# Pins, grouped routing and interleaved first expert products in a fused attention and two-layer expert kernel

## The chip, the cores and the metric

The kernel runs on one core of one Trainium2 chip. The metric is device time in microseconds (us) of one execution. Lower is better. The core has TensorE (PE, matrix products), VectorE (DVE), ScalarE (ACT), GpSimd (POOL) and SyncE (SP, which issues most of the transfers). Each engine runs its own instructions in one fixed order and waits for the others by semaphores.

## The reference, cut to what matters

Three layers follow one another on 3072 tokens of 512 values.

```python
# 1. attention, 4 x 8 heads of 64: 8 global keys and a causal window of 96, with a linear bias
a = softmax(where(keep, q @ k.T / 8 + bias, -1e9)); x = (a @ v)              # [3072, 512]
# 2. a dense pair of layers
h = x @ w_in;  g = where(h > 0, h, exp(min(h, 0)) - 1);  y = g @ w_out       # 512 -> 2048 -> 512
# 3. eight experts, the best one for each token that is to be computed at all
chosen = y @ w_skip > 0;  logits = y[chosen] @ w_gate;  e = argmax(logits)
gate = softmax(logits)[e]
out = y;  out[chosen] += gate * (relu(y @ w1[e]) @ w2[e])                    # 512 -> 1024 -> 512
```

## The kernel before, in words

**Groups and steps.** The 3072 tokens are 24 tiles of 128, in eight groups `m` of three tiles. For each group, `program` (L807) walks over sixteen slices `f` of the 2048 hidden values. One step `(m, f)` issues `moe_h(m, f)` (L429: twelve products of 384 columns, then ScalarE, VectorE, ScalarE and GpSimd in a chain that makes the half-precision pair `gs`) and, two steps behind it (`LAG`, L50), `moe_y` (L451: nine products of 512 columns). Between the steps of groups 0 to 6 stand pieces of the attention of the next group (`att_step`, L357). Numbers are split into two half-precision parts, so that each product is made of three.

**The check of the first weights.** The weights of the layer pair arrive as pairs of 32-bit words and are rebuilt in `w_prep` (L399) during group 0. Later they are loaded a second time and checked: 16 loads of 1 MB (`w_load(f, "wc")`, L393) and 32 VectorE operations (`w_check`, L419, the operation on L425), of which the program text has one every second step of groups 2 to 5 (L889 to L893). A load is written down four steps ahead of its first check, the very first one two steps ahead. The loads use the two buffers `stage`, which the expert weights use later (L595).

**Routing.** `route(m)` (L488) returns pieces that later steps call one by one: `evac` copies the three results out of PSUM, `turn` splits a tile and turns it by a transposing transfer, `gate` makes nine logits for one tile (eight products into `lg`, then eleven VectorE operations and one ScalarE exponential, per tile), `place` counts ranks with two products into `rk` and finds each token's slot with twelve VectorE operations per tile, `scatter` writes a tile's rows into the DRAM tensor `xg` by an indirect transfer from GpSimd. Scatters into one tensor wait for each other. `write` copies the last group's rows to the output.

**The experts.** `ex_tail` (L681) has steps too. Steps 0 to 47 take the first 128 slots of experts 0, 1 and 2 (steps 0 to 23) and then their second 128 slots (steps 24 to 47), eight slices each; after them come experts 3 to 7. A step issues `ex_first` (L638, twelve products), one weight split per tile (`prep`, L848, which calls `ex_prep`, L603) and, two steps behind, `ex_second` (L658, three products per tile). The rows of a tile come from `xg` by `ex_gather` (L620) and are split and turned by `ex_tokens` (L628): two VectorE operations (L634, L635) into the single buffer `yh`, then a transposing transfer into `eyT`. The routing pieces of the last group stand between these steps, by `ROUTE_LAST` (L60). When an expert's tile is done, L674 makes the result, L676 turns the token number into an index `ix` (two buffers, L675), and L677 scatters the rows to the output.

**What sets the order.** The program text isn't the order on the engines. A scheduler at build time simulates the kernel and puts on each engine what is ready first by its own times; an operation whose inputs it takes as early can be put far ahead of its place in the text. `pin` (L72) prevents that: a pinned instruction comes behind the one that was written just before it on its engine. It adds order, not a wait. Before the change the ScalarE half of each weight split is pinned (L613), but not the loads and operations of the check, nor L634.

Of the kernel before, what the change touches and what calls it, by code (L numbers as in the profile page):

```python
# [19 lines left out]
P = 128  # L20
# [39 lines left out]
ROUTE_LAST = {0: 'et', 4: 'A', 5: 'B', 6: 'C', 8: 'p', 9: 'sw'}  # L60


class Fast:
# [424 lines left out]
    def route(self, m):  # L488

        nc, mp = self.nc, self.mp  # L490
        sm = mp.tile([P, TB, 32], F32, tag="sm", name=f"sm_{m}", bufs=2)
        oh = mp.tile([P, TB, E], F16, tag="oh", name=f"oh_{m}", bufs=2)
        yts, yTs, poss = {}, {}, {}
# [24 lines left out]

        def gate(t):
            n = m * TB + t  # L520
            yt = yts[t]
            lg = self.ps.tile([P, 2, E + 1], F32, tag=f"s{t % 2}", name=f"lg_{n}", bufs=1)
# [4 lines left out]
            q = sm[:, t, :]  # L527
            L = mp.tile([P, E + 1], F32, tag="L", name=f"L_{n}", bufs=2)
            nc.vector.tensor_scalar(L, lg[:, 1, :], 1.0 / (RS * GS), None, ALU.mult)
            nc.vector.scalar_tensor_tensor(L, lg[:, 0, :], 1.0 / (RS * GS), L, ALU.mult, ALU.add)  # L530
            m8 = mp.tile([P, 8], F32, tag="m8", name=f"m8_{n}", bufs=2)
            mi = mp.tile([P, 8], U32, tag="mi", name=f"mi_{n}", bufs=2)
            nc.vector.max(m8, L[:, 0:E])
            nc.vector.max_index(mi, m8, L[:, 0:E])

            nc.vector.tensor_scalar(q[:, 0:1], m8[:, 0:1], -1.0, None, ALU.mult)
            nc.scalar.activation(q[:, 8:16], L[:, 0:E], AF.Exp, bias=q[:, 0:1], accum_out=q[:, 1:2])

            nc.vector.scalar_tensor_tensor(q[:, 7:8], L[:, E:E + 1], 0.0, q[:, 1:2], ALU.mult, ALU.add)
            nc.vector.tensor_tensor(self.esum[:, t:t + 1], self.esum[:, t:t + 1], q[:, 7:8], ALU.add)  # L540
            nc.vector.tensor_copy(q[:, 2:3], mi[:, 0:1])
            nc.vector.tensor_scalar(q[:, 3:4], L[:, E:E + 1], 0.0, None, ALU.is_gt)
            nc.vector.tensor_scalar(oh[:, t, :], self.iota8, q[:, 2:3], q[:, 3:4], ALU.is_equal, ALU.mult)

        def place():
            rk = self.ps.tile([P, 2, TB, E], F32, tag="s1", name=f"rk_{m}", bufs=1)
            for x in range(2):
                nc.tensor.matmul(rk[:, x], self.tri[:, x, :], oh, start=True, stop=True)
            for t in range(TB):
                n = m * TB + t  # L550
                q, yt = sm[:, t, :], yts[t]
                nc.vector.tensor_tensor(q[:, 16:24], rk[:, 0, t, :], self.carry, ALU.add)
                nc.vector.tensor_tensor_reduce(q[:, 24:32], q[:, 16:24], oh[:, t, :], 1.0, 0.0,
                                               ALU.mult, ALU.add, q[:, 4:5])
                nc.vector.tensor_tensor(self.carry, self.carry, rk[:, 1, t, :], ALU.add)
# [125 lines left out]
    def ex_tail(self, prep):  # L681
# [8 lines left out]
        for s_, (e, f, tiles) in enumerate(steps):  # L690
# [23 lines left out]
            for _ in tiles:  # L714
                prep()
# [457 lines left out]
```

## Time and profile before

| | |
|---|---|
| median of 3 runs | 878.21 us (876.48 to 879.97) |
| the profiled execution | 877.69 us; its span on the chip 876.0 us |
| PE busy | 818.5 us, 93% |
| DVE, ACT, POOL busy | 604.8, 535.9, 176.3 us |
| mean granted TensorE clock | 0.978 of full speed |
| moved by transfers | 148.80 MB, mean 170 GB/s |
| the sixteen DMA engines' share for SP's transfers | 62.6% |

A share is a mean over stages that differ: attention and weight loading at first, the steady steps of the layer pair in the middle, the experts at the end. The stretches below are given in us from the start of the span. Group 1 ends its results with the evacuation at 248.5 us, and the last group with that at 678 us.

### The profile page before, as it was taken

To read this page: it belongs to the slowest core of one execution; us is meant where nothing else is said; L and a number is where in the kernel's file an instruction comes from. 1 tells how busy PE (TensorE), PEld (TensorE's weight loads), DVE (VectorE), ACT (ScalarE), POOL (GpSimd) and SP (SyncE) were. 2 spreads that over 40 slices of the span, in tenths; PEclk is the share of its full clock that TensorE was granted. 3 is DMA by queue.
4 is the path that set the end of the run, shared out by engine and by line. 5 is a ranking of instruction groups with operands and counts; after the bars stand their busy time and mean duration, and the time that the engine had idled before them with its cause. 6 is when DMAs were issued, how large, how long until landed. Compare 5 with 4: busy or idle time off the path is not lost.

```text
span 876.0 us, 17838 instructions
## 1 busy us (share of the span) xinstructions
PE 818.5 (93%) x6177; PEld 476.3 (54%) x6177; DVE 604.8 (69%) x2263; ACT 535.9 (61%) x1326; POOL 176.3 (20%) x201
## 2 busy tenths in 40 slices
PE   6998888889999999999999999999998879999995
PEld 5774444445555555555555555555553646766663
DVE  6997897778767647756755765652786957876632
ACT  4775766566777767777767777654665635554311
POOL 1001112112312322312231231132232011100100
PEclk9998899899999999999999999999999999999998
DMA  8999999999875445457546543630546787878410
GB/s 290 270 281 263 223 268 254 249 268 312 212 142 112 109 121 120 113 103 155 114 96 115 109 78 69 111 65 13 168 147 185 225 247 240 263 241 239 134 43 25
DMA packets 185396, 148.80 MB, mean 170 GB/s; under 512 B 152209, under 2 KB 154257, under 8 KB 181201
## 3 DMA queue, kind: packets, MB, share of 16 engines
q1 hardware_dynamic: 182096, 141.59, 62.6%
q0 software_dynamic: 3200, 5.99, 1.9%
q8 instruction: 50, 0.82, 0.4%
q14 instruction: 50, 0.40, 0.2%
HBM read 94.82 MB, written 21.08 MB: 132 GB/s over the span
## 4 chain that ended last, share of the span: by engine, by line
PE 61%; DMA 13%; DVE 12%; issue 11%; POOL 1%; ACT 1%; SPq 0%; POOLq 0%; DVEq 0%; ACTq 0%
PE h L437 23%; PE y L458 21%; PE s L239 5%; DMA out<-eres,ix 5%; PE pv L324 4%; PE eh L650 3%; PE eo L666 3%; DMA xg<-yt,pos 2%; PE warm L354 2%; DMA yTs<-yh 1%; DVE wt L406 1%; DVE wt L407 1%; DMA wc<-in_wf 1%; DVE e L444 1%; DVE w L414 1%
## 5 line engine op out<-in xcount | busy, mean ns | idle before, releaser
L437 PE MATMUL h<-xT,w 128*128 128x384 f16 x1536 | 277.2, 331 | 5.3 <-DMA xT<-xs 3.6
L458 PE MATMUL y<-w,gs 128*128 128x512 f16 x1152 | 271.5, 380 | 3.7 <-POOL gs L448 1.9
L448 POOL TENSOR_TENSOR gs<-e,gs 128x384 f16<-128x384 f32 x128 | 126.8, 992 | 420.0 <-ACT gs L447 364.9
L437 PEld LDWEIGHTS <-w 128*128 128x128 f16 x1536 | 147.4, 99 | 109.4 <-issue 13.7
L458 PEld LDWEIGHTS <-gs 128*128 128x128 f16 x1152 | 110.5, 98 | 125.1 <-POOL gs L448 3.4
L447 ACT ACTIVATE gs<-e 128x384 f16<-128x384 f32 x128 | 66.9, 523 | 97.2 <-DVE e L444 96.3
L444 DVE SCALAR_TENSOR_TENSOR e<-e,h 128x384 f32<-128x384 f32 x128 | 70.5, 551 | 73.7 <-ACT e L442 71.0
L253 ACT ACTIVATE p<-p,st 128x232 f32<-128x232 f32 (+1 forms) x192 | 89.3, 466 | 39.8 <-DVE st L248 39.5
L666 PE MATMUL eo<-ew,ehs 128*128 128x512 f16 x384 | 101.7, 385 | 6.7 <-DVE ehs L654 6.6
L650 PE MATMUL eh<-eyT,ew 128*128 128x128 f16 (+1 forms) x1152 | 101.8, 239 | 4.9 <-DMA eyT<-eyh 3.4
L650 PEld LDWEIGHTS <-ew 128*128 128x128 f16 x1152 | 86.8, 99 | 31.3 <-issue 5.5
L614 DVE SCALAR_TENSOR_TENSOR ew<-er,ew 128x512 f16<-128x512 f32 x128 | 88.8, 711 | 9.3 <-ACT ew L613 8.6
L441 ACT ACTIVATE e<-h 128x384 f32<-128x384 f32 x128 | 61.5, 480 | 45.7 <-PE h L437 38.5
L652 ACT ACTIVATE ehs<-eh 128x128 f16<-128x128 f32 (+1 forms) x96 | 30.0, 312 | 96.1 <-PE eh L650 93.5
L248 DVE CUSTOM_DVE_ANT_0 p<-s,tab 128x232 f32<-128x232 f32 (+1 forms) x192 | 67.1, 376 | 18.4 <-PE s L239 15.8
L613 ACT ACTIVATE ew<-er 128x512 f16<-128x512 f32 x128 | 75.5, 620 | 6.7 <-DMA er<-in_moe_w 6.6
L283 DVE TENSOR_TENSOR ph<-p,ph 128x464 f16<-128x464 f32 x68 | 44.2, 663 | 39.5 <-ACT ph L282 39.5
L442 ACT ACTIVATE e<-e 128x384 f32<-128x384 f32 x128 | 66.7, 521 | 3.2
L666 PEld LDWEIGHTS <-ehs 128*128 128x128 f16 x384 | 35.1, 99 | 33.4 <-DVE ehs L654 10.7
L239 PE MATMUL s<-qh 64*128 64x232 f16 (+1 forms) x432 | 40.9, 257 | 10.9 <-DVE st L248 8.4
L654 DVE SCALAR_TENSOR_TENSOR ehs<-eh,ehs 128x128 f16<-128x128 f32 (+1 forms) x96 | 31.7, 331 | 26.0 <-ACT ehs L652 26.0
L677 POOL DMA_INDIRECT out<-eres,ix x16 | 17.1, 1069 | 144.9 <-DVE eres L674 112.5
(172 smaller groups left out, 915.1 us busy)
## 6 DMA issues: line engine op xcount, KB each, us to landing
er<-in_moe_w SPq DMA_DIRECT2D x64, 512.0 KB
wr<-in_wf SPq DMA_DIRECT2D x16, 1024.0 KB
wc<-in_wf SPq DMA_DIRECT2D x16, 1024.0 KB
qk<-in_qk SPq DMA_DIRECT2D x20, 720.0 KB
out<-yt SPq DMA_DIRECT2D x24, 256.0 KB
rawv<-in_vp SPq DMA_DIRECT2D x21, 256.0 KB
xg<-zrow SPq DMA_DIRECT2D x16, 257.0 KB
yg<-xg SPq DMA_DIRECT2D x16, 257.0 KB
```

Source lines behind the costliest of these rows:

```text
L239: nc.tensor.matmul(sp[j], q[r, hp, KW:], k[r, hp, KW - w:KW], start=(x == 0), stop=(x == len(mm) - 1))
L248: nc.vector.tensor_tensor_reduce(pw[:, j, :], sp[j], self.tab[:, h, :] if i else self.tab0[:, h, :], -0.125, 3e38, ALU.add, ALU.min, st[:, ...
L253: nc.scalar.activation(pw[:, j, :], pw[:, j, :], AF.Exp, bias=st[:, 0, h:h + 1], scale=-1.0, accum_out=st[:, 1, h:h + 1])
L437: nc.tensor.matmul(hps, wi[:, s_, c, :], xT[:, x * ND + c, :], start=(n == 0), stop=(n == 3 * ND - 1))
L444: nc.vector.scalar_tensor_tensor(g, e, -HS, hps, ALU.mult, ALU.max, accum_out=self.gsum[:, m * NF + f:m * NF + f + 1])
L447: nc.scalar.activation(gs[:, 0], g, AF.Copy)
L448: nc.gpsimd.tensor_tensor(gs[:, 1], g, gs[:, 0], ALU.subtract)
L458: nc.tensor.matmul(self.ys[m][t], gs[:, s_, t * P:(t + 1) * P], wo[:, x, :], start=(f == 0 and n == 0), stop=(f == NF - 1 and n == 2))
L613: self.pin(nc.scalar.activation(w[:, 0], r, AF.Copy, scale=sc))
L614: nc.vector.scalar_tensor_tensor(w[:, 1], r, sc, w[:, 0], ALU.mult, ALU.subtract, accum_out=self.esums[:, c:c + 1])
L650: nc.tensor.matmul(hps, l, r, start=(i == 0), stop=(i == len(mm) - 1))
L666: nc.tensor.matmul(self.eo[(e, t)], hs[:, s_, j * P:(j + 1) * P], self.ew[(e, 4 + f // 2, f % 2)][:, x, :], start=(f == 0 and n == 0), sto ...
```

## The change

Six edits. (1) The check's loads and operations, and L634, are pinned. (2) The routing's VectorE work is done for three tiles in one operation where it can be; the logits leave PSUM by a ScalarE copy, and the exponential is one operation for three tiles, off the way to the slots. (3) The ranks come from nine products of eight columns instead of two of 24, so that the sum over earlier tiles of the group is made in PSUM. (4) The last two `moe_y` steps of the layer pair move behind the expert steps' first products: steps 0 and 1, `moe_y(7, 14)`, step 2, `moe_y(7, 15)`. For that steps 0 to 2 take their PSUM from `s0`, `s1` and `h` in turn. (5) The routing pieces of the last group, and what follows from them, come three steps later, the second tiles' tokens two steps later. (6) `ix` has 16 buffers.

```diff
-ROUTE_LAST = {0: 'et', 4: 'A', 5: 'B', 6: 'C', 8: 'p', 9: 'sw'}
+ROUTE_LAST = {3: 'et', 7: 'A', 8: 'B', 9: 'C', 11: 'p', 12: 'sw'}
...
-        self.nc.sync.dma_start(t, self.a["wf"].bitcast(I32)[f].rearrange("p k (d t) -> p k d t", t=2))
+        d = self.nc.sync.dma_start(t, self.a["wf"].bitcast(I32)[f].rearrange("p k (d t) -> p k d t", t=2))
+        if name == "wc":
+            self.pin(d)
...
-        self.nc.vector.scalar_tensor_tensor(self.andw, self.wc[:, k, :, 1], 0x40000000, self.andw,
-                                            ALU.bitwise_xor, ALU.bitwise_and)
+        self.pin(self.nc.vector.scalar_tensor_tensor(self.andw, self.wc[:, k, :, 1], 0x40000000, self.andw,
+                                                     ALU.bitwise_xor, ALU.bitwise_and))
...
+            nc.scalar.activation(Lr[:, t], lg, AF.Copy, scale=1.0 / (RS * GS))
+            if t == TB - 1:
+                choose()
+
+        def choose():
+            L = mp.tile([P, TB, E + 1], F32, tag="L", name=f"L_{m}", bufs=2)
+            nc.vector.tensor_tensor(L, Lr[:, :, 0, :], Lr[:, :, 1, :], ALU.add)
...
+            for t in range(TB):
+                nc.vector.max(m8[:, t], L[:, t, 0:E])
+                nc.vector.max_index(mi[:, t], m8[:, t], L[:, t, 0:E])
+            nc.vector.tensor_copy(expert, mi[:, :, 0])
+            nc.vector.tensor_scalar(chosen, L[:, :, E], 0.0, None, ALU.is_gt)
+            nc.vector.tensor_tensor(oh, self.iota8.unsqueeze(1).to_broadcast([P, TB, E]), wide(expert), ALU.is_equal)
+            nc.vector.tensor_tensor(oh, oh, wide(chosen), ALU.mult)
...
+            nc.scalar.activation(z, z, AF.Exp)
+            nc.vector.tensor_reduce(out=esum, in_=z, op=ALU.add, axis=AX.X)
...
+            rk = self.ps.tile([P, TB + 1, E], F32, tag="s1", name=f"rk_{m}", bufs=1)
+            for t in range(TB + 1):
+                for x in range(min(t + 1, TB)):
+                    nc.tensor.matmul(rk[:, t], self.tri[:, 0 if x == t else 1, :], oh[:, x],
+                                     start=(x == 0), stop=(x == min(t, TB - 1)))
...
+            nc.vector.tensor_tensor(z, rk[:, 0:TB], self.carry.unsqueeze(1).to_broadcast([P, TB, E]), ALU.add)
+            nc.vector.tensor_tensor(self.carry, self.carry, rk[:, TB], ALU.add)
+            nc.vector.tensor_tensor(z, z, oh, ALU.mult)
+            nc.vector.tensor_reduce(out=rank, in_=z, op=ALU.add, axis=AX.X)
+
+            nc.vector.scalar_tensor_tensor(check, rank, float(CAP), chosen, ALU.is_lt, ALU.mult)
+            nc.vector.tensor_scalar(check, check, -OOB, OOB, ALU.mult, ALU.add)
+            nc.vector.scalar_tensor_tensor(slot, expert, float(CAP), rank, ALU.mult, ALU.add)
+            nc.vector.tensor_tensor(pos, slot, check, ALU.add)
...
-        nc.vector.tensor_scalar(yh[:, 0], y, RS, None, ALU.mult)
+        self.pin(nc.vector.tensor_scalar(yh[:, 0], y, RS, None, ALU.mult))
...
-            ix = self.xp.tile([P, 1], I32, tag="ix", name=f"ix_{e}_{t}", bufs=2)
+            ix = self.xp.tile([P, 1], I32, tag="ix", name=f"ix_{e}_{t}", bufs=2 * E)
...
-            if s_ == 10:
+            if s_ == 0:
+                self.htags = "s0", "s1", "h"
+            if s_ == 3:
+                self.htags = ("h",)
+            if s_ == 13:
                 self.htags = "h", "s0", "h", "s1"
-            if s_ == 12:
+            if s_ == 15:
                 for x in range(NX):
                     self.ex_gather(x, 1)
             for x in range(NX):
-                if s_ == 20 + 2 * x:
+                if s_ == 22 + 2 * x:
                     self.ex_tokens(x, 1)
...
             self.ex_first(e, f, tiles)
+            if s_ and rest:
+
+                self.moe_y(*rest.pop(0))
...
-        for k in range(LAG):
-            self.moe_y(*steps[k - LAG])
-        self.ex_tail(prep)
+        self.ex_tail(prep, steps[-LAG:])
```

## Rows read from the trace of the kernel before

**Rows 1.** Windows: each engine's busy us (x instructions), granted clock, DMA share, GB/s.

```profile
136.00:167.00 31.00, 25.93 (x163) 12.96 (x161) 21.14 (x59) 17.95 (x46) 6.38 (x6) 0.89 0.86 250
167.00:249.00 82.00, 77.74 (x578) 41.53 (x577) 63.16 (x227) 55.25 (x137) 19.73 (x19) 0.98 0.96 245
249.00:322.00 73.00, 72.92 (x559) 39.45 (x557) 47.76 (x194) 52.51 (x135) 19.23 (x19) 1.00 0.51 120
615.00:679.00 64.00, 60.33 (x341) 30.85 (x340) 46.80 (x186) 39.54 (x84) 17.20 (x18) 1.00 0.55 171
```

**Rows 2.** Windows of the check's operation alone, L425 on DVE.

```profile
136.00:167.00 31.00, 9.55 (x12) 0.89 0.86 250
167.00:249.00 82.00, 15.03 (x20) 0.98 0.96 245
```

**Rows 3.** Timeline of ACT: evacuations; start, us, line, op, tiles, count [idle before].

```profile
167.54 1.07 ACT L499 ACTIVATE yt<-y 128x512 f32<-128x512 f32 x2
248.54 1.07 ACT L499 ACTIVATE yt<-y 128x512 f32<-128x512 f32 x2
322.49 1.07 ACT L499 ACTIVATE yt<-y 128x512 f32<-128x512 f32 x2
```

**Rows 4.** Timeline of DVE: a check behind a load that is late.

```profile
153.96 0.69 DVE L425 SCALAR_TENSOR_TENSOR andw<-wc,andw 128x512 int32<-128x512 int32 x1 [6.01 <-DMA wc<-in_wf]
```

**Rows 5.** Windows behind the idle time of PE that ends at 156 us.

```profile
156.00:160.00 4.00, 3.90 (x14) 1.67 (x14) 3.38 (x12) 3.11 (x10) 0.67 (x1) 0.50 0.75 252
160.00:165.00 5.00, 5.00 (x30) 2.29 (x29) 2.47 (x10) 2.84 (x6) 0.56 (x1) 0.79 1.00 277
```

**Rows 6.** Timeline of DVE: token splits at the end of the layer pair.

```profile
660.58 0.43 DVE L634 TENSOR_SCALAR eyh<-yg 128x512 f16<-128x512 f32 x1 [3.73 <-DMA yg<-xg]
664.96 1.12 DVE L634 TENSOR_SCALAR eyh<-yg 128x512 f16<-128x512 f32 x1 [0.71 <-DMA eyT<-eyh]
```

**Rows 7.** Chain of waits: start, us, what; products, and a gather's landing.

```profile
577.20 0.04 PE rk L548 x2
696.20 0.67 PE eh L650 x12
696.87 0.65 PE eo L666 x3
708.89 2.70 DMA yg<-xg
```

**Rows 8.** Timeline of POOL: the last group's three scatters.

```profile
694.86 0.99 POOL L572 DMA_INDIRECT xg<-yt,pos  x1 [17.25 <-DVE sm L557]
700.34 0.97 POOL L572 DMA_INDIRECT xg<-yt,pos  x1 [4.48 <-ACT ew L613]
705.76 1.37 POOL L572 DMA_INDIRECT xg<-yt,pos  x1 [3.18 <-DMA out<-eres,ix]
```

**Rows 9.** Timeline of DVE: index and token splits in the experts' first steps.

```profile
705.47 0.15 DVE L676 CAST ix<-yg 128x1 int32<-128x1 f32 x1 [5.03 <-DMA out<-eres,ix]
718.86 0.43 DVE L634 TENSOR_SCALAR eyh<-yg 128x512 f16<-128x512 f32 x1 [2.81 <-issue]
```

**Rows 10.** Timeline of DVE: an index that waits, later experts.

```profile
792.21 0.15 DVE L676 CAST ix<-yg 128x1 int32<-128x1 f32 x1 [3.58 <-DMA out<-eres,ix]
```

**Rows 11.** Timeline of PE: products that began after idle time.

```profile
677.67 1.68 PE L458 MATMUL y<-w,gs 128*128 128x512 f16 x7 [0.39 <-POOL gs L448]
720.77 0.39 PE L666 MATMUL eo<-ew,ehs 128*128 128x512 f16 x1 [2.18 <-DVE ehs L654]
798.29 1.48 PE L650 MATMUL eh<-eyT,ew 128*128 128x256 f16 x12 [1.72 <-DMA eyT<-eyh]
820.96 1.47 PE L650 MATMUL eh<-eyT,ew 128*128 128x256 f16 x12 [1.65 <-DMA eyT<-eyh]
```

**Rows 12.** Groups by line: shapes xcount | busy us, mean ns | idle before, releasers.

```profile
L530 DVE SCALAR_TENSOR_TENSOR L<-lg,L 128x9 f32<-128x9 f32 x24 | 4.0, 167 | 0.6
L537 ACT ACTIVATE sm<-L,sm 128x8 f32<-128x8 f32 x24 | 7.2, 298 | 8.9 <-DVE sm L536 8.6
```

More of the change, by code (lines that the diff above doesn't have):

```diff
@@ L490, in route @@
         nc, mp = self.nc, self.mp
-        sm = mp.tile([P, TB, 32], F32, tag="sm", name=f"sm_{m}", bufs=2)
+        sm = mp.tile([P, 7, TB], F32, tag="sm", name=f"sm_{m}", bufs=2)
         oh = mp.tile([P, TB, E], F16, tag="oh", name=f"oh_{m}", bufs=2)
-        yts, yTs, poss = {}, {}, {}
+        pos = mp.tile([P, TB], I32, tag="pos", name=f"pos_{m}", bufs=2)
+        Lr = mp.tile([P, TB, 2, E + 1], F32, tag="Lr", name=f"Lr_{m}", bufs=2)
+        esum, expert, chosen, rank, slot, check, gate_ = (sm[:, x, :] for x in range(7))
+        yts, yTs = {}, {}
         def evac():
@@ L517, in turn, with wide @@
             nc.sync.dma_start_transpose(yTs[t], yh.rearrange("p s d -> p (s d)"))
+        def wide(x):
+            return x.unsqueeze(2).to_broadcast([P, TB, E])
         def gate(t):
-            n = m * TB + t
-            yt = yts[t]
-            lg = self.ps.tile([P, 2, E + 1], F32, tag=f"s{t % 2}", name=f"lg_{n}", bufs=1)
+            lg = self.ps.tile([P, 2, E + 1], F32, tag=f"s{t % 2}", name=f"lg_{m}_{t}", bufs=1)
             for c in range(ND):
@@ L526, in gate @@
                 nc.tensor.matmul(lg[:, 0, :], yTs[t][:, ND + c, :], self.wgs[:, c, 0, :], start=False, stop=(c == ND - 1))
[L527 to L541, printed above, removed]
@@ L542, in gate @@
-            nc.vector.tensor_scalar(q[:, 3:4], L[:, E:E + 1], 0.0, None, ALU.is_gt)
-            nc.vector.tensor_scalar(oh[:, t, :], self.iota8, q[:, 2:3], q[:, 3:4], ALU.is_equal, ALU.mult)
-        def place():
[L546 to L555, printed above, removed]
-                nc.vector.tensor_scalar(q[:, 5:6], q[:, 4:5], float(CAP), None, ALU.is_lt)
-                nc.vector.tensor_tensor(q[:, 5:6], q[:, 5:6], q[:, 3:4], ALU.mult)
-                nc.vector.tensor_scalar(q[:, 5:6], q[:, 5:6], -OOB, OOB, ALU.mult, ALU.add)
-                nc.vector.scalar_tensor_tensor(q[:, 6:7], q[:, 2:3], float(CAP), q[:, 4:5], ALU.mult, ALU.add)
-                nc.vector.tensor_tensor(q[:, 6:7], q[:, 6:7], q[:, 5:6], ALU.add)
-                pos = mp.tile([P, 1], I32, tag="pos", name=f"pos_{n}", bufs=4)
-                nc.vector.tensor_copy(pos, q[:, 6:7])
-                nc.vector.tensor_scalar(q[:, 1:2], q[:, 1:2], 1e-9, RS * E1S * E2S, ALU.add, ALU.mult)
-                nc.vector.reciprocal(yt[:, DM:DM + 1], q[:, 1:2])
-                poss[t] = pos
@@ new lines, in gate @@
+            nc.scalar.activation(Lr[:, t], lg, AF.Copy, scale=1.0 / (RS * GS))
[4 more added lines that the diff above has]
+            nc.vector.tensor_tensor(L, Lr[:, :, 0, :], Lr[:, :, 1, :], ALU.add)
+            m8 = mp.tile([P, TB, 8], F32, tag="m8", name=f"m8_{m}", bufs=2)
+            mi = mp.tile([P, TB, 8], U32, tag="mi", name=f"mi_{m}", bufs=2)
+            for t in range(TB):
[5 more added lines that the diff above has]
+            nc.vector.tensor_tensor(oh, oh, wide(chosen), ALU.mult)
+            z = mp.tile([P, TB, E], F32, tag="z", name=f"z_{m}", bufs=2)
+            nc.vector.tensor_tensor(z, L[:, :, 0:E], wide(m8[:, :, 0]), ALU.subtract)
+            nc.scalar.activation(z, z, AF.Exp)
+            nc.vector.tensor_reduce(out=esum, in_=z, op=ALU.add, axis=AX.X)
+            nc.vector.scalar_tensor_tensor(check, L[:, :, E], 0.0, esum, ALU.mult, ALU.add)
+            nc.vector.tensor_tensor(self.esum, self.esum, check, ALU.add)
+            nc.vector.tensor_scalar(gate_, esum, 1e-9, RS * E1S * E2S, ALU.add, ALU.mult)
+            for t in range(TB):
+                nc.vector.reciprocal(yts[t][:, DM:DM + 1], gate_[:, t:t + 1])
@@ L572, in scatter @@
             nc.gpsimd.indirect_dma_start(
-                out=self.xg[:, :], out_offset=bass.IndirectOffsetOnAxis(ap=poss[t].bitcast(U32)[:, 0:1], axis=0),
+                out=self.xg[:, :], out_offset=bass.IndirectOffsetOnAxis(ap=pos.bitcast(U32)[:, t:t + 1], axis=0),
                 in_=yts[t][:, :], in_offset=None, bounds_check=E * CAP - 1, oob_is_err=False)
@@ L679, in ex_second, with ex_tail @@
                 in_=r[:, :], in_offset=None, bounds_check=NT - 1, oob_is_err=False)
-    def ex_tail(self, prep):
+    def ex_tail(self, prep, rest):
         both = tuple(range(CAP // P))
```

1 line of the change is left out of this document (added).

## The prediction

> **What bounds the kernel now.** Begin with the windows, because a mean over the whole span hides the stages [rows 1]. From 249 us on, PE is busy for 72.92 of 73 us: a steady group of the layer pair is bound by PE, with DVE busy 65% and the transfers at half of their share. Three stretches differ. From 136 to 167 us PE stands still for 5.07 us and the clock is granted at 0.89; from 167 to 249 us it lacks 4.3 us, with the transfers at 0.96; from 615 to 679 us it lacks 3.67 us.
>
> Then ask what DVE does in the first two that it doesn't do in the third. The check's operation runs there 32 times, 24.58 us together, and after 249 us not at all [rows 2], though the program text has it in groups 2 to 5. The scheduler took the loads as early and moved the whole check ahead by about a hundred us. What that does is seen at one place: a check waits 6.01 us for its load and holds every later DVE operation [rows 4], attention's among them, so PE runs dry. Behind that, the clock falls to the lower of its two levels, 1.2 GHz, from 156 to 160 us, and averages 0.79 up to 165 us [rows 5]. The evacuations give the price over a whole group: group 1 takes 81.00 us from one to the next, group 2 takes 73.95 [rows 3].
>
> The third view is the end. There DVE does the same thing with token splits, which wait 3.73 us for a gather ahead of the layer pair's own work [rows 6], and with `ix`, which waits for an output scatter because it has two buffers: 5.03 us and 3.58 us [rows 9, 10]. The last `moe_y` ends at 679.35 us; PE stands still before step 24 (2.18 us) and in the later experts (1.72 and 1.65 us) [rows 11].
>
> **The change, part by part.** Against the profiled execution, 877.69 us (span 876.0 us and 1.7 us around it); the median is 0.5 us above it.
>
> *The check.* With pins, a check stands behind the DVE work of its own step, so the 24.58 us of DVE and the 16 MB leave the stretch from 124 to 249 us. The stall goes: 5.07 us. The lost clock goes: half of 3.90 us and 0.21 of 5.0 us [rows 5], 3.0 us. Group 1 becomes a steady group: 81.00 - 73.95 = 7.05 us. Together 15.1 us. What is late next there is PE itself, as in group 2. Where they go, the checks add 24.58 us of DVE over four groups, 296 us, to a busy share of 65%, so 74%, and 16 MB add about 55 GB/s to 120. The cover is PE's own work; without it a check would cost what it does now, 7.05 us for 20 of them, 11 us for 32. Bounds 0 and 11 us; I take 1 us, near zero, because PE keeps 77.74 of 82 us even in the stretch where the checks are three times as dense and the transfers twice as busy.
>
> *The end of the layer pair.* Pinned token splits come behind the weight splits of step 13, when the gather has long landed [rows 6], so the DVE wait ahead of the pair goes. The last two steps' chains through ACT, DVE and POOL are covered by three first products of 0.67 us [rows 7], 2.0 us of work from behind. The 3.67 us of idle time become work, less the 2.0 us moved in: the last `moe_y` ends 1.7 us sooner, at 677.7 us. Bounds 0 and 3.7 us.
>
> *Step 24.* It needs the second tile of expert 0, which waits for the last group's routing: evacuation, gates, ranks, three scatters, gather, split, transfer. Moving the pieces three steps later leaves them at the same distance from the last `moe_y`, since three steps' products now lie before it. Today the first scatter comes 15.5 us behind that end. Grouped DVE work saves some of it: 8 operations instead of 36 in `place`, but the ranks still wait for the third gate. Bounds 0 and 2.5 us; I take 1.0, near the lower, since weight splits lie between those operations anyway. From the first scatter to the gather's issue are 14.0 us [rows 7, 8]. One scatter takes from 3.1 us (the third) to 5.5 us (the first), so three take 9.4 to 16.4; I take 13.0, a little under 14.0, because the third waited behind an output scatter that will now have gone ahead. The gather lands in 2.70 us. From there to the free `yh` buffer, that is split and transfer, are 7.3 us now (711.6 to 718.86 [rows 9]) and 4.4 us in the quiet stretch [rows 6]; I take 5.8, the middle, because the transfers will be as busy as now, but no index blocks them. Together 14.5 + 13.0 + 2.7 + 5.8 = 36.0 us, so step 24 starts at 713.7 us; now it starts at 721.0, just behind the product at 720.77. Gain 7.3 us, the 1.7 us above included. PE's own work needs only 0.65 + 21 steps of 1.32 us [rows 7] + 0.8 us for gates and ranks, 29.2 us: **it will stand still for some 7 us before step 24**, where today it stands in several shorter pieces. An idle time of 5.07 us cost 3.0 us of clock [rows 5]; today's 2.18 us I take for half of that, so 1.5 us are lost here. Bounds of the step: a gain of 14 us (no wait) and of 1.5 us (41.9 us after 677.7).
>
> *Behind step 24.* With 16 buffers no index waits. The 1.72 and 1.65 us went to splits and weights that stood on DVE behind such indices [rows 10, 11]: gain 3.4 us. What is late next is the result's own buffer, two deep, but its scatter has a whole tile's time. Bounds 0 and 3.4 us.
>
> *Small costs.* Two rank products take 0.04 us on the chain [rows 7], so nine take 0.2 us; seven groups, and the eighth inside step 24's chain: 1.2 us on PE. The copies of logits to ACT: one exponential of the same size took 298 ns, the two DVE operations they replace about 167 ns each [rows 12]. ACT loses two exponentials per group and gains three copies, hidden under the following `moe_y`. On SP, the last group's output rows are now written down behind expert 0's output scatter, to the same tensor; they and the weight loads queued behind wait for it, up to 5.5 us, which two steps of loaded weights cover. I take 0, and the upper bound into the range.
>
> The sum: -15.1 - 7.3 - 3.4 + 1.0 + 1.5 + 1.2 = -22.1 us; 855.6 us, and 0.5 us up to the median: **856 us**.
>
> **Rivals.** *No wait at step 24.* If scatters go at their fastest and transfers are quiet, the chain takes 30 us and PE's own 29.2 decide: 7 us less, 3 us of clock not lost, the 1 us for the checks too: 845 us. For it speaks the third scatter; against it, three scatters in a row took 14 us here.
>
> *Loads that come late.* The pinned load is issued only four steps ahead, the first only two, and SP runs in order, behind transfers that wait for DVE. If it comes late, each check waits as the one in rows 4 does, but in groups 2 to 5, and the 15.1 us return: 871 us. Four steps are over 15 us (a group of sixteen takes 73.95), and the transfers are half idle there, which speaks against it. The Trainium skill, DMA: Bandwidth & Descriptors, Rules for kernel authors, advises issuing a transfer early and waiting for it late. The change issues later than before; by that rule the sum would be this one, and rows 4, where an early issue itself blocked DVE, don't bear it out.
>
> *The pins move nothing.* A pin ties an operation to the one written before it, and that one may itself float ahead. Then the checks stay: 871 us. Against it: the one before is mostly a step's own L444, which PE releases.
>
> *Slower: gates that hold PE.* The logits' PSUM is attention's `s0` or `s1`. It is now freed by ScalarE, in order behind its other work. For eighteen gates (groups 0 to 5) the next scores stand behind one `moe_y`, nine products, 1.95 us by rows 7. If ScalarE came 6.0 us late, as it would behind a DVE stall like that of rows 4, each gate would cost 4.05 us, 73 us in all: 929 us. It decides from 1.5 us per gate. Against it: ScalarE stood idle 8.9 us over 24 exponentials, waiting for them [rows 12]. The Trainium skill, ScalarE: Activation LUTs, Rules for kernel authors, wants add and multiply on VectorE, not ScalarE. By durations alone the rows show no loss in it.
>
> **How the numbers follow.** My forecast has 0.62, with its own range 848 to 866; no wait at step 24 has 0.14; a chain later still (861 us) 0.05; late loads 0.10; unmoved checks 0.05; slow gates 0.04. A measurement here tells about 0.5%, 4.4 us. All but the last lie below 873.8 us, and the two at 871 us can end above it: faster 0.93, same 0.03, slower 0.04. The range leaves out the slow gates, most of the two at 871 and a little below: 844 to 869.
>
> **What would show it.** L425 spread over 237 to 500 us, without waits over 1 us; an evacuation distance of about 74 us for group 1, with the first evacuation 8 us sooner. First products among the last `moe_y`. One idle time of 5 to 9 us at step 24, behind `eyT`, with the clock down behind it. No wait at L676. Wrong would be: L425 still before 200 us; scores idle behind `lg`; idle time at the last `moe_y` that stays; or PE running through step 24.

## The result, and the profile after

| | before | changed |
|---|---|---|
| median | 878.87 us (876.48 to 879.97, 4 runs) | 866.22 us (864.51 to 866.86, 4 runs) |
| the profiled execution, its span | 877.69 us, 876.0 us | 866.19 us, 864.5 us |
| evacuation of group 6 | 614.73 us | 601.33 us |
| step 24 starts | 720.99 us | 713.55 us |
| PE's last product ends | 866.2 us | 855.5 us |

The ratio of the times is 0.9875 (95% interval 0.9848 to 0.9901): faster by 1.25%, a small step but clear of the noise, and 12.65 us where 22.1 were forecast. The rows of the table cut the 11.5 us of the profiled execution into four: 13.4 us are gained up to the evacuation of group 6, **6.0 us are lost from there to step 24** (106.26 us before, 112.22 now), 3.3 us are gained from step 24 to the last product (145.2 and 141.9), and 0.8 behind it.

Windows of the changed kernel (stretch, length, then busy us of PE, PEld, DVE, ACT and POOL, granted clock, DMA share, GB/s):

```profile
136.00:159.00 23.00, 22.96 (x151) 11.92 (x150) 14.02 (x48) 17.61 (x45) 5.62 (x6) 1.00 0.45 104
159.00:233.00 74.00, 73.61 (x575) 40.09 (x573) 43.04 (x154) 52.43 (x131) 18.95 (x19) 1.00 0.55 128
233.00:307.00 74.00, 73.92 (x570) 39.95 (x569) 48.62 (x164) 52.82 (x134) 18.72 (x19) 1.00 0.67 175
602.00:668.00 66.00, 63.44 (x385) 34.77 (x383) 43.98 (x151) 41.19 (x88) 17.09 (x18) 0.97 0.58 170
706.00:717.00 11.00, 6.94 (x40) 4.14 (x41) 6.91 (x28) 1.49 (x4) 0.97 (x1) 0.50 1.28 289
```

The first two answer to the bad stretches of [rows 1]: PE now runs through both, at the full clock. In the last one, around step 24, PE works at half the clock, 1.2 GHz, for 11 us. The kernel before had a milder form of it: 11 us from its own step 24 on, the clock was granted at 0.84:

```profile
720.00:731.00 11.00, 10.23 (x99) 7.20 (x100) 9.17 (x37) 4.77 (x12) 1.16 (x1) 0.84 0.79 245
```

ACT's timeline of the changed kernel (start, us, line, tiles), the first evacuations of groups 0, 1, 2, 6 and 7, and behind it the check's line in the view of one line:

```profile
159.14 1.07 ACT L504 ACTIVATE yt<-y 128x512 f32<-128x512 f32 x2
234.11 1.07 ACT L504 ACTIVATE yt<-y 128x512 f32<-128x512 f32 x2
308.01 1.06 ACT L504 ACTIVATE yt<-y 128x512 f32<-128x512 f32 x2
601.33 1.06 ACT L504 ACTIVATE yt<-y 128x512 f32<-128x512 f32 x2
666.67 1.78 ACT L504 ACTIVATE yt<-y 128x512 f32<-128x512 f32 x3
```

```profile
L427 DVE SCALAR_TENSOR_TENSOR andw<-wc,andw x32: 683/686/690, 238.7 to 527.9; 128x512 int32<-128x512 int32 x32
```

Against [rows 3] the first evacuation comes 8.4 us sooner and group 1 takes 74.97 in place of 81.00 us. The checks lie between 238.7 and 527.9 us. Under that line the view names no idle time ahead of any of them, where [rows 4] had 6.01 us.

PE's timeline of the changed kernel at the end: the last `moe_y`, gate A (the first logits products of the last group), and products behind idle time. Below it, ACT's evacuation of group 6 and PE's gate A and step 24 in the kernel before.

```profile
660.11 2.68 PE L660 MATMUL eh<-eyT,ew 128*128 128x128 f16 x24 [2.56 <-DMA eyT<-eyh]
665.71 2.11 PE L460 MATMUL y<-w,gs 128*128 128x512 f16 x9
673.11 0.83 PE L660 MATMUL eh<-eyT,ew 128*128 128x128 f16 x12 [2.00 <-DVE ehs L664]
677.40 0.25 PE L530 MATMUL lg<-wgs,yTa 128*128 128x18 f16 x4
706.09 1.46 PE L676 MATMUL eo<-ew,ehs 128*128 128x512 f16 x3 [4.88 <-DVE ehs L664]
713.55 4.00 PE L660 MATMUL eh<-eyT,ew 128*128 128x128 f16 x36 [3.09 <-DMA eyT<-eyh]
```

```profile
614.73 1.07 ACT L499 ACTIVATE yt<-y 128x512 f32<-128x512 f32 x2
685.36 0.26 PE L524 MATMUL lg<-wgs,yTa 128*128 128x18 f16 x4 [0.87 <-DMA yTa<-yha]
720.99 0.83 PE L650 MATMUL eh<-eyT,ew 128*128 128x128 f16 x12
```

The last `moe_y` ends at 667.8 us, 66.5 us behind the evacuation of group 6; before it was 64.6 (679.35 by [rows 11], less 614.73). Gate A follows 9.6 us later, where it was 6.0. PE then stands twice, 4.88 us ahead of step 23's second product and 3.09 us ahead of step 24. The 1.72 and 1.65 us of the later experts [rows 11] are gone; a new idle time of 1.93 us stands at 736 us, where DVE holds a token split that waits for its gather.

DVE's timeline (index casts and the split for step 24), and POOL's (the three scatters), both of the changed kernel:

```profile
645.69 0.15 DVE L686 CAST ix<-yg 128x1 int32<-128x1 f32 x1 [3.85 <-DMA yg<-xg]
705.67 0.15 DVE L686 CAST ix<-yg 128x1 int32<-128x1 f32 x1 [6.78 <-DMA yg<-xg]
707.20 0.42 DVE L644 TENSOR_SCALAR eyh<-yg 128x512 f16<-128x512 f32 x1
```

```profile
689.11 0.97 POOL L582 DMA_INDIRECT xg<-yt,pos  x1 [3.20 <-ACT ew L623]
696.32 0.98 POOL L582 DMA_INDIRECT xg<-yt,pos  x1 [6.24 <-DMA xg<-yt,pos]
700.07 0.97 POOL L582 DMA_INDIRECT xg<-yt,pos  x1 [2.77 <-ACT ehs L662]
```

With 16 buffers the cast no longer waits for an output scatter [rows 9]. The build has hoisted it to right behind the gather, and there it waits for the gather, at the head of DVE.

### The profile page after: what moved, and what is told of

It reads as the page before. It is cut to its first block, busy times and chain, and to the rows that moved or that the text cites. A ratio compares the mean times of both kernels' runs of the same rounds, so it can differ in the third digit from the quotient of the medians.

```text
span 864.5 us, 17637 instructions
## 1 busy us (share of the span) xinstructions
PE 817.8 (95%) x6233; PEld 479.4 (55%) x6233; DVE 571.4 (66%) x1951; ACT 530.0 (61%) x1310; POOL 174.5 (20%) x201
## 4 chain that ended last, share of the span: by engine, by line
PE 72%; DVE 11%; DMA 10%; issue 4%; POOL 1%; ACT 1%; SPq 0%; POOLq 0%; DVEq 0%; ACTq 0%
PE h L439 25%; PE y L460 24%; PE eh L660 7%; PE eo L676 6%; PE s L239 5%; PE pv L324 4%; DMA eyT<-eyh 3%; DMA xg<-yt,pos 2%; DMA yg<-xg 2%; DVE ew L624 2%; DVE wt L408 2%; DVE wt L409 1%; PE warm L354 1%; DMA xT<-xs 1%; DVE w L416 1%
## 5 line engine op out<-in xcount | busy, mean ns | idle before, releaser
L660 PE MATMUL eh<-eyT,ew 128*128 128x128 f16 (+1 forms) x1152 | 103.6, 243 | 7.6 <-DMA eyT<-eyh 5.6
L660 PEld LDWEIGHTS <-ew 128*128 128x128 f16 x1152 | 88.7, 101 | 32.8 <-issue 6.7
L624 DVE SCALAR_TENSOR_TENSOR ew<-er,ew 128x512 f16<-128x512 f32 x128 | 90.5, 725 | 15.9 <-ACT ew L623 14.5
```

Of the source, the lines that this page charges most:

```text
L624: nc.vector.scalar_tensor_tensor(w[:, 1], r, sc, w[:, 0], ALU.mult, ALU.subtract, accum_out=self.esums[:, c:c + 1])
L660: nc.tensor.matmul(hps, l, r, start=(i == 0), stop=(i == len(mm) - 1))
```

## The experiments

Each kernel ran beside the kernel before on its chip, which took 874.97 to 876.47 us on these chips; so times are given as ratios to it. Its trace is from another chip, where it took 878.87 us: places in two traces can differ by such an amount. Lengths within a trace differ less: groups 2 to 6 take 367.2 us in both traces of the changed kernel. "Behind" counts from the end of the last `moe_y`; "changed again" is the changed kernel, for a ratio beside the others.

> The changed kernel itself, for a ratio on the same chip as the three below it and against more runs of the kernel before. Every theory: the ratio of the first measurement, 0.9875, within its interval of 0.985 to 0.990.

| kernel | median us | ratio (95%) | evacuation 6 | from it to step 24 | gate A behind | 1st scatter behind | step 24 behind | step 24 to end |
|---|---|---|---|---|---|---|---|---|
| before | 878.87 | 1 | 614.7 | 106.3 | 6.0 | 15.5 | 41.6 | 145.2 |
| changed | 866.22 | 0.9875 | 601.3 | 112.2 | 9.6 | 21.3 | 45.7 | 141.9 |
| changed again | 864.11 | 0.9862 (0.9837 to 0.9887) | 601.6 | 109.3 | 9.9 | 21.6 | 45.2 | 143.4 |
| checks only | 873.38 | 0.9994 (0.9975 to 1.0013) | 610.5 | 106.8 | 5.6 | 16.0 | 42.4 | 144.0 |
| checks undone | 877.26 | 1.0022 (1.0004 to 1.0040) | 612.7 | 109.4 | 10.4 | 22.0 | 46.0 | 140.9 |
| not interleaved | 860.20 | 0.9835 (0.9811 to 0.9858) | 602.2 | 105.8 | 6.8 | 17.4 | 42.4 | 141.3 |
| casts pinned | 871.82 | 0.9972 (0.9954 to 0.9990) | 602.0 | 108.1 | 10.3 | 22.0 | 45.8 | 150.7 |
| splits free | 863.02 | 0.9873 (0.9852 to 0.9894) | 600.5 | 107.7 | 9.3 | 21.3 | 45.2 | 144.3 |
| not interleaved, two buffers | 864.81 | 0.9866 (0.9838 to 0.9893) | 601.1 | 105.4 | 6.6 | 17.1 | 41.0 | 148.8 |
| not interleaved, first splits free | 857.63 | 0.9798 (0.9771 to 0.9825) | 601.8 | 104.9 | 6.3 | 17.1 | 41.5 | 139.8 |
| pieces sooner | 863.84 | 0.9853 (0.9828 to 0.9877) | 603.1 | 107.9 | 6.0 | 18.0 | 41.5 | 142.5 |
| casts behind | 858.66 | 0.9790 (0.9763 to 0.9817) | 602.4 | 104.3 | 6.3 | 17.2 | 42.0 | 141.8 |
| gathers behind | 853.99 | 0.9765 (0.9750 to 0.9780) | 601.7 | 100.1 | 6.6 | 17.3 | 37.8 | 140.7 |
| changed, gathers behind | 863.10 | 0.9846 (0.9820 to 0.9873) | 602.0 | 109.2 | 9.6 | 21.3 | 42.9 | 140.8 |

### Where the early gain comes from

**The checks alone**, on the kernel before; and, in a later group, **the checks undone**, on the changed one. Up to 640 us nothing of the change acts but the pins of the check and the grouped routing.

```diff
 # checks only: the kernel before, with
+        if name == "wc":
+            self.pin(d)
-        self.nc.vector.scalar_tensor_tensor(self.andw, ...
+        self.pin(self.nc.vector.scalar_tensor_tensor(self.andw, ...
 # checks undone: the changed kernel without these lines
```

> The kernel before, with the pins on the check and on its load alone; the end is the old one. Theory (all that the change gains lies in the early part, the rest of it nets about nothing): 865 us, 13 to 14 below the kernel before, as the evacuation at 601 us of the changed kernel was 13.4 us ahead of the old one; first evacuation near 159 us, group 1 near 75 us, L425 spread from 238 to 528 us without waits; the end as before (2.2 us idle at step 24, 1.7 and 1.65 us behind the index casts). Rival (the early gain is partly given back behind it, since loads, splits or scatters of the end don't move with PE): 869 to 872 us.

> The changed kernel without the pins on the check and on its load; grouped routing, interleaving, 16 index buffers and pinned splits stay. With the checks alone, the evacuation of group 6 came at 610.5 us, 4.2 ahead of the kernel before, and with checks and grouped routing at 601.3. Theory of an interaction (36 narrow DVE operations per group leave no room for the moved checks; without the checks there is room and grouping pays little): group 6's evacuation at 611 to 614 us, groups 2 to 5 at 73.9 to 74.5 each, and a ratio to the kernel before of 0.997 to 1.002. Rival (the two add: grouping is worth 9 us by itself): group 6's evacuation near 605 us, ratio 0.992 to 0.994.

Neither number of the first was met: alone, the pins gain nothing that a ratio shows (0.9994). They do all that they are meant to do: first evacuation at 159.96 us, group 1 in 75.3 us, checks from 239.8 us on. But groups 2 to 6 then take 375.2 us, from one of the first two evacuations below to the other, where before they took 366.2 and in the changed kernel 367.2. The other two are those of the checks undone.

```profile
235.27 1.07 ACT L501 ACTIVATE yt<-y 128x512 f32<-128x512 f32 x2
610.51 1.07 ACT L501 ACTIVATE yt<-y 128x512 f32<-128x512 f32 x2
```

```profile
245.62 1.06 ACT L502 ACTIVATE yt<-y 128x512 f32<-128x512 f32 x2
612.65 1.06 ACT L502 ACTIVATE yt<-y 128x512 f32<-128x512 f32 x2
```

Windows of one slow group of the checks alone, and of the same group of the changed kernel's repeated run:

```profile
461.60:540.30 78.70, 76.61 (x573) 41.22 (x572) 55.00 (x209) 54.00 (x135) 18.54 (x19) 0.98 0.62 147
```

```profile
457.20:532.20 75.00, 74.88 (x580) 40.69 (x579) 50.83 (x170) 53.25 (x133) 19.13 (x19) 1.00 0.67 153
```

With routing tile by tile DVE has 209 instructions and is busy for 55.0 us of that group, with grouped routing 170 and 50.8. What waits is seen in the summary of PE's waits over groups 2 to 6 of the checks alone, which in the changed kernel is empty:

```profile
PE s L239 <- DVE st L248: 5.7, 6, 1.8
PE rk L550 <- DVE st L248: 0.5, 2, 0.3
```

Attention's scores stand behind a softmax step that DVE does too late; these two waits are 6.2 of the 9.0 us. With the checks undone and the rest in place, the theory of an interaction holds: the evacuation of group 6 comes at 612.7 us, 11.1 us behind the changed kernel's on the same chip, groups 2 to 6 take 367.0 us, and the ratio is 1.0022. (The traced execution, 874.05 us, is the fastest of its twelve; the median is 877.26.) So the grouped routing gains little without the checks, 2.1 us at the evacuation of group 6, and the checks little without the grouped routing: the one makes the room on DVE that the other fills. An operation of one tile, 128x1, took 0.13 to 0.17 us in the kernel before; one of all three tiles, 128x3 (L573 to L575), takes 0.15 to 0.17.

### What made step 24 late

**Not interleaved**: the changed kernel with the last two `moe_y` ahead of the experts again.

```diff
-ROUTE_LAST = {3: 'et', 7: 'A', 8: 'B', 9: 'C', 11: 'p', 12: 'sw'}
+ROUTE_LAST = {0: 'et', 4: 'A', 5: 'B', 6: 'C', 8: 'p', 9: 'sw'}
-            if s_ and rest:
-                self.moe_y(*rest.pop(0))
+        for k in range(LAG):
+            self.moe_y(*steps[k - LAG])     # ahead of ex_tail; gathers at 12, splits at 20 + 2 * x
```

> The changed kernel with the last products of the layer pair again ahead of all the first products of the experts, and the pieces of the last route at their old steps; pins, grouped routing and 16 index buffers stay. Theory (the move of the first products is what made the chain to step 24 longer: it brings gate A from 6.0 to 9.7 us behind the last moe_y, and the first scatter from 15.5 to 21.4): first scatter 14.5 to 16 us behind the last moe_y, step 24 some 38 to 40 us behind it in place of 45.9, time 860 to 863 us. Rival (the index casts, hoisted behind the gathers, are what held the chain): the distance stays at 43 us or more, the DVE waits of 3.9 and 6.8 us stay, time 865 to 868 us. Second rival (the move pays after all, as the diff's order suggests): idle time of 3 to 4 us at the last moe_y returns and the time is 869 us or more.

860.2 us, as the theory has it. POOL's first scatter and PE's step 24:

```profile
682.93 1.44 POOL L582 DMA_INDIRECT xg<-yt,pos  x1 [19.77 <-DVE eres L684]
707.99 1.04 PE L660 MATMUL eh<-eyT,ew 128*128 128x128 f16 x12 [2.79 <-DMA eyT<-eyh]
```

The first scatter is back at 17.4 us and step 24 comes 105.8 us behind the evacuation of group 6, against 112.2 and 109.3; the distance of 38 to 40 us was too hopeful (42.4). The intervals of the two ratios, 0.9835 and 0.9862, overlap; the 3.5 us to the repeat are the traces' finding. The edit undoes two things at once, the interleaving and the later pieces; the next run moves the pieces alone.

**Pieces sooner**: interleaved, with each piece of the last route one step earlier.

```diff
-ROUTE_LAST = {3: 'et', 7: 'A', 8: 'B', 9: 'C', 11: 'p', 12: 'sw'}
+ROUTE_LAST = {3: 'et', 6: 'A', 7: 'B', 8: 'C', 10: 'p', 11: 'sw'}     # gathers 14, splits 21 + 2 * x
```

> The changed kernel with the gates, the ranks, the scatters, the gathers and the splits of the second tiles one step sooner; the first products stay interleaved. In the repeated run of the changed kernel gate A came 9.9 us behind the last moe_y, against 6.0 in the kernel before, and between them lay four first and four second products, against four and two. Theory (the chain to step 24 is as long as the work that the program text puts ahead of each of its pieces, and a step is 1.3 us): gate A at 8.5 to 9 us, the first scatter 1.3 to 2 us nearer to the last moe_y (about 20 in place of 21.6), step 24 at 43 to 44.3 in place of 45.2, ratio 0.983 to 0.986 against 0.9862. Rival (the chain is bound by the transposing transfer of the last group's rows, which gate A then waits for): PE idles 1 us or more ahead of gate A and the distances stay within 0.5 us.

PE doesn't wait ahead of gate A, so the rival falls, and gate A, the scatter and step 24 move nearer by more than the theory says (6.0, 18.0, 41.5 us): the place of the pieces, with the waiting and the clock that go with it, sets the chain's length even with the products interleaved. The time stays (0.9853): in that run the last `moe_y` itself came 66.3 us behind the evacuation of group 6 in place of 64.0, with 2.29 us of idle time for `eyT` and the clock at 0.80 to 0.85 from 660 to 670 us. Placed ahead of the last `moe_y`, the first products bring a wait for their own tokens with them.

**Splits free**: the token splits of the changed kernel without their pin.

```diff
-        self.pin(nc.vector.tensor_scalar(yh[:, 0], y, RS, None, ALU.mult))
+        nc.vector.tensor_scalar(yh[:, 0], y, RS, None, ALU.mult)
```

> The changed kernel with the token splits free to be hoisted, as in the kernel before. Theory (the pin costs 2.6 us at step 0, where expert 0's first tile is now split 8.7 us after its gather landed, and gains little, since the index casts wait for that gather in the same place anyway): the PE idle of 2.6 us at step 0 goes, DVE waits about 3.9 us for the gather as it does now, time 863 to 866 us. Rival (the pin is what lets the last layers run through): DVE's wait grows and PE stands 3 to 4 us at the last moe_y; 868 to 870 us.

Step 0 no longer waits, the last `moe_y` comes 62.5 us behind the evacuation, and 863.0 us is within the theory; but the ratio is that of the changed kernel. The pins on splits, all together, change nothing here that the ratio shows.

**First splits free**: the two joined, with the pin left on the later splits.

```diff
-        self.pin(nc.vector.tensor_scalar(yh[:, 0], y, RS, None, ALU.mult))
+        d = nc.vector.tensor_scalar(yh[:, 0], y, RS, None, ALU.mult)
+        if t or e >= NX:
+            self.pin(d)                     # and not interleaved, as above
```

> The changed kernel with the first products not interleaved, and with the splits of the first tiles of experts 0 to 2 free to be hoisted (the later ones stay pinned). Theory (pinned, the second of these splits waits 0.7 us at the head of DVE for the transfer before it, in front of the last L446, and PE stands 2.2 us at the last moe_y for it; free, it is ahead of that): the 2.2 us go, ratio 0.980 to 0.983. Rival (as in the kernel before, the free splits wait for their gather in front of the pair's own work): 2 to 4 us of idle time at the last moe_y stay, ratio 0.983 to 0.987.

0.9798, below the changed kernel's interval on the same chip, and at the theory's edge. Yet the 2.2 us at the last `moe_y` stay, as the rival has it (1.04, 0.38, 0.52 and 0.39 us). What these splits gain over the kernel that isn't interleaved is not settled: the two intervals overlap.

### The index casts

**Casts pinned**: the cast kept in program order, in the changed kernel.

```diff
-            nc.vector.tensor_copy(ix, y[:, DM + 1:DM + 2])
+            self.pin(nc.vector.tensor_copy(ix, y[:, DM + 1:DM + 2]))
```

> The changed kernel with one edit: the index cast is kept behind the operation traced before it. Theory (the cast, hoisted to right behind the gather by the build, holds DVE 3.9 us at 645 and 6.8 us at 706 us, and the split of the second tile stands behind others by then): both waits go; the split starts within 0.5 us of the gather's landing instead of 1.5; the 4.9 us of PE idle before step 23 goes or moves to step 24; step 24 comes 2 to 3 us sooner; 862 to 864 us. Rival (DVE's wait costs nothing, since whatever stands behind it waits for the same gather in the end): step 24 stays within 0.7 us, 865.5 to 867 us. If instead the whole miss of 13 us lay in these waits: 853 to 856 us.

The rival is right on step 24, which stays at 45.8 us. DVE's timeline shows why, PE's what no theory had:

```profile
702.29 0.43 DVE L644 TENSOR_SCALAR eyh<-yg 128x512 f16<-128x512 f32 x1 [5.40 <-DMA yg<-xg]
```

```profile
788.77 2.74 PE L660 MATMUL eh<-eyT,ew 128*128 128x256 f16 x12 [5.60 <-DMA eyT<-eyh]
815.47 1.47 PE L660 MATMUL eh<-eyT,ew 128*128 128x256 f16 x12 [3.51 <-DMA eyT<-eyh]
```

The split takes the cast's place and waits for the same gather. And from step 24 to the end it takes 150.7 us, 871.8 in all: the cast is also a reader of the gathered row. Pinned, it starts up to 1.9 us behind the start of `eres`, keeps the row's buffer that long, and the next gather with it, which is then issued together with another and with weight loads. SP's timeline with the casts pinned (two gathers in one line), and in the changed kernel:

```profile
769.46 0.94 SPq L635 DMA_DIRECT2D yg<-xg  x2
```

```profile
774.20 0.33 SPq L635 DMA_DIRECT2D yg<-xg  x1
776.08 0.33 SPq L635 DMA_DIRECT2D yg<-xg  x1
```

With the casts pinned no cast waits, so the 8.8 us against the changed kernel's first trace (7.3 against the repeat) aren't a wait of DVE for an output scatter. How the later gathers become PE's 5.60 and 3.51 us is read from the order of the issues; no run shows it by itself. The early cast is a gain behind step 24 even where it waits ahead of it.

**Two buffers** again, not interleaved.

```diff
-            ix = self.xp.tile([P, 1], I32, tag="ix", name=f"ix_{e}_{t}", bufs=2 * E)
+            ix = self.xp.tile([P, 1], I32, tag="ix", name=f"ix_{e}_{t}", bufs=2)
```

> The changed kernel with the first products not interleaved (0.9835 of the kernel before), and with two index buffers again. Theory (the early cast is worth something behind step 24, because it frees the gathered row's buffer and so the next gather; with the cast pinned late, that stretch took 150.7 us in place of 141.9): from step 24 to the end 144 to 146 us in place of 141.3, DVE waits of 3 to 5 us for an output scatter, ratio 0.987 to 0.990. Rival (the buffers are worth nothing, since DVE waits for the gather in place of the scatter): ratio 0.982 to 0.985.

As the theory has it, and more: 148.8 us in place of 141.3 behind step 24. The ratio, 0.9866, is just under the theory's, and its interval overlaps that of 0.9835, so the 7.5 us, too, are the traces' finding. The summary of DVE's waits from 700 us on:

```profile
DVE ix L686 <- DMA out<-eres,ix: 17.3, 9, 4.3
DVE eyh L644 <- DMA yg<-xg: 6.2, 4, 2.4
```

Here the casts wait for output scatters again, as before the change, so this run by itself doesn't tell that wait from a row's buffer that comes free late; the run with the casts pinned does.

**Casts behind**: only the casts of the second tiles of experts 0 to 2 pinned.

```diff
+            if e < NX and t:
+                self.pin(d)                 # d: the cast; on top of "first splits free"
```

> The fastest so far (first products not interleaved, first tiles' splits free; 0.9798 of the kernel before) with the index casts of the second tiles of experts 0 to 2 kept in program order; the others stay free to be hoisted. There the hoisted cast holds DVE 6.0 us for the gather, and the split that step 24 needs starts 3.7 us behind the gather's landing, behind what had piled up. Theory (the cast's wait does cost there, unlike in the interleaved kernel, where the split stood close behind the gather either way): the split starts within 0.5 us of the landing, step 24 comes 3 us sooner (38 to 39 us behind the last moe_y in place of 41.5), ratio 0.974 to 0.978. Rival (as with all the casts pinned, a late cast keeps the gathered rows' buffers and makes later gathers late): step 24 sooner, but 3 us or more lost behind it, ratio 0.980 or more.

The split starts at the gather's landing, and step 24 comes no sooner, 42.0 us. SP's timeline (issues), and the windows behind it:

```profile
696.72 0.42 SPq L635 DMA_DIRECT2D yg<-xg  x1
697.25 0.60 SPq L610 DMA_DIRECT2D er<-in_moe_w  x1
698.30 3.83 SPq L648 DMA_TRANSPOSE eyT<-eyh  x1
```

```profile
697.00:700.00 3.00, 1.51 (x16) 0.77 (x13) 1.24 (x4) 0.00 (x0) 0.00 (x0) 1.00 0.94 307
700.00:703.00 3.00, 0.00 (x0) 0.00 (x0) 0.00 (x0) 0.54 (x2) 0.00 (x0) 0.68 0.98 332
```

The transposing transfer is 3.83 us in its issue, with the transfers at 0.94 and 0.98 of their share: what bounds step 24 now is the queue, and the last gather ahead of it, issued at 696.72 us, is for expert 3, whose first split comes at step 43.

### The queue ahead of step 24

**Gathers behind**, on the last kernel, and the same on the changed one.

```diff
-                for x in range(NX):
-                    self.ex_gather(x, 1)
+                self.ex_gather(0, 1)
+            if s_ == 20:                    # 22 in the changed kernel; splits 4 steps apart
+                for x in range(1, NX):
+                    self.ex_gather(x, 1)
+        if e == NX or (t and 0 < e < NX):   # in ex_gather
+            self.pin(d)
```

> As the run with the casts behind (0.979), with three gathers moved: of the second tiles only expert 0's is gathered ahead of step 24's split, those of experts 1 and 2 are issued behind its transposing transfer, and expert 3's are kept in their own place; the splits of experts 1 and 2 come at steps 24 and 28. In that run the split stood right behind the gather, but its transfer was 3.8 us in the issue in place of 1.2, with the transfers at 0.94 to 1.23 of their share from 697 to 707 us, and step 24 came no sooner (41.95 us behind the last moe_y). Theory (what binds step 24 there is the queue: four gathers and three weight loads are in front of a transfer that PE waits for): issue back at 1.2 us, split to step 24 in 5.5 to 7 us in place of 9.7, step 24 at 38 to 40 us, ratio 0.974 to 0.977. Rival (the weight loads alone fill the queue, or gathers that come later make later experts late): distance within 1 us of 41.95, or from step 24 to the end over 143 us; ratio 0.978 or more.

> The changed kernel (0.9862 in its repeated run) with the same move of gathers alone: experts 1 and 2's second tiles are gathered behind the transposing transfer that step 24 waits for, expert 3's in their own place; splits at steps 22, 26, 30; casts free, first products interleaved. Theory (in the changed kernel the queue is only a small part of what makes step 24 late, since the split came 1.5 us behind the gather and the transfer took 5.1 us; most lies ahead of the first scatter): step 24 at 43 to 44.5 us behind the last moe_y in place of 45.2, ratio 0.983 to 0.987. Rival (the queue is the main cause): step 24 at 41 us or less, ratio under 0.981.

Both go by their theories, to within 0.3 us. SP's and PE's timelines of the first:

```profile
697.82 1.24 SPq L650 DMA_TRANSPOSE eyT<-eyh  x1
```

```profile
701.77 1.44 PE L664 MATMUL eh<-eyT,ew 128*128 128x128 f16 x12 [1.61 <-DMA eyT<-eyh]
```

The issue is back at 1.24 us, split to step 24 takes 5.2 us, step 24 comes 37.8 us behind the last `moe_y`, though three weight loads still lie ahead of the transfer (the last 3.1 us ahead of it, 1.1 in the run before). **853.99 us, 0.9765, beats both kernels**; against the run with the casts behind the intervals overlap, and the 4.2 us at step 24 are the traces' finding. In the changed kernel the same move brings step 24 to 42.9 us, though not the time out of its interval: there most of the delay lies ahead of the first scatter. The Trainium skill, DMA: Bandwidth & Descriptors, section Queues, rings and completion order, says that on each DMA engine descriptors are consumed in ring order. The two rows of the transposing transfer, 3.83 us in the issue behind four gathers and 1.24 us behind one, fit that.

## Why the prediction was right or wrong

**The check: the number was right, its reason half.** Forecast 15.1 us gained and 1 us paid for the new place; measured 13.4 (8.4 at the first evacuation, 6.0 in group 1, 1.0 lost in groups 2 to 6). The checks were also said to be three times as dense in the stretch from 167 to 249 us as in their new place; they are 2.3 times (20 in 82 us, 32 in 296). But the text names PE's own work as the cover of the moved checks, and counts the grouped routing at nothing there. The runs show the cover to be the room that grouping makes on DVE: without it the new place costs 9.0 us (375.2 against 366.2), near the upper bound of 11 that the text gave. That the 1 us came out is owed to an edit to which the text gave no part in it, and so to luck.

**Step 24: the step that failed.** "Moving the pieces three steps later leaves them at the same distance from the last `moe_y`" was wrong, and so the term of -7.3 us became +6.0. The forecast put step 24 at 713.7 in the old kernel's times, 99.0 us behind the evacuation of group 6; it came 112.2 us behind. The 13.2 us are: the last `moe_y` 3.5 later than forecast (66.5 against 63.0), the first scatter 6.8 (21.3 against 14.5), the scatters up to the gather's issue 0.8 (13.8 against 13.0), the gather nothing (2.7), split and transfer 2.1 (7.9 against 5.8). In the repeat they are 1.1, 7.1, 0.1 and, for gather, split and transfer, 2.0; of the first run's 3.5 us at the last `moe_y`, 0.8 are longer idle time at step 0 and 1.6 the clock behind it.

The 6.8 us are 3.6 up to gate A, 2.2 from gate A to the scatter (11.7 against 9.5) and the 1.0 that grouping was to save. On the 3.6: the text counted steps, but a step grows on the way. Gate A stood behind four first and two second products, of 0.67 and 0.65 us [rows 7], and 1.8 us of idle time, 6.0 us. Three steps later it stands behind four and five, 2.0 us in which a first product waits for DVE's six splits of the last group, and 1.7 us by which the products from 673.8 to 677.4 us took longer at the lower clock (0.53 there), 9.6 us. One step sooner, with three and four products, a wait of 1.38 us and the full clock, it was 6.0.

With the old order the scatter is back at 17.4, still 1.4 to 1.9 us later than in the checks alone and in the kernel before. Of that, 1.2 and 0.8 us lie ahead of gate A; from gate A to the scatter are 10.5 us, against 10.4 and 9.5. So grouping saved nothing here that the traces show, though it leaves fewer operations. The first scatter now waits for all three tiles' positions, while the third comes at the same distance (26.4 us in the kernel before and in the one not interleaved); what that wait costs by itself no run shows.

The sum comes out nearly whole once two things that it didn't count are out of the way, the casts at the head of DVE and the gathers ahead of the transfer. In the run with the gathers behind, which has the old order of pieces too, the chain takes 17.3 us to the first scatter, 12.1 to the gather's issue, and from there to step 24 8.5, as forecast: 37.8 in place of 36.0.

**The end of the pair.** The DVE wait was to go and the last `moe_y` to come 1.7 us sooner. The idle time at the last `moe_y` did go; in its place step 0 waits 2.56 us (1.75 in the repeat), since its pinned split starts 8.7 us behind the gather's landing, at 654.4 and 645.7 us. In the first run the clock is granted at 0.66 from 660 to 665 us.

**Behind step 24: right.** No cast waits for an output scatter, and 3.3 us are gained (1.8 in the repeat), where 3.4 less 1.5 of clock were forecast. Why was not seen: the cast that waits early frees the gathered row's buffer early. "No index waits" was false as a sentence, since it now waits for gathers, 3.85 and 6.78 us. That wait costs nothing at step 24 in the changed kernel (45.8 us with the casts pinned).

**The rivals.** No wait at step 24 fell with PE's two idle times there. Gates that hold PE fell: between 178 and 657 us PE idles nowhere, though ScalarE frees the logits. Late loads and unmoved pins fell with the view of L427: issued later, the loads and checks cost groups 2 to 6 0.2 us (367.2 against 367.0 with the checks undone), not 15. A later chain was right in kind and too small in price, 861 us. In the last two runs gathers issued later bring step 24 4.2 and 2.3 us nearer. The Trainium skill, DMA: Bandwidth & Descriptors, Rules for kernel authors, advises issuing a transfer early; these rows don't bear that out for the check's loads and for the gathers.

## What to carry to other kernels

Count the distance of a moved piece in the work that its engine does ahead of it, not in loop steps, and look at each queue for what stands in front: a wait at the head of an engine that runs in fixed order, or gathers ahead of the one transfer that PE needs. Where an edit fills an engine and another empties it, ask for each what it is worth without the other. A small operation that reads a buffer last decides when it comes free.

## What was not expected of the hardware

A transposing transfer's issue took 1.24 us in one kernel and 3.83 us in another, with the transfers at 0.94 of their share, and SP stood with it. The first gather of a batch landed in 2.7 us; the last of four, with weight loads between them, took 7.2 us in the changed kernel (705.3 to 712.5) and 7.7 in the one with the casts behind (696.7 to 704.4). And idle times at the same place had different effects on the clock: behind 2.56 us, ending at 660 us, it was granted at 0.66 over the next 5 us, behind 1.75 us in the repeat at 1.00.
